# Value products of an attention with mixed heads: three pairs of heads at a time in one PSUM bank, and a third bank for the mixed scores

## The chip, the cores and the metric

One core of a Trainium2 chip runs the whole program. The metric is the device time of one execution in microseconds (us). The engines are named as the profile names them: PE is the matrix engine (PEld its weight loads), DVE the vector engine, ACT the scalar engine, POOL GpSimd, and SP the engine that issues most DMAs. A matmul's result lies in PSUM, which has eight banks; DVE and ACT read it from there.

## The reference, cut to what matters

```python
scores = scale * np.matmul(q, k.transpose(0, 1, 3, 2))     # 2 batches, 12 heads, 448 x 448, depth 64
scores = np.einsum('bhij,hg->bgij', scores, w_pre)         # heads are mixed before the softmax
attn = np.exp(scores - np.max(scores, axis=-1, keepdims=True))
attn = attn / (np.sum(attn, axis=-1, keepdims=True) + 1e-09)
attn = np.einsum('bhij,hg->bgij', attn, w_post)            # and after it
x = np.matmul(attn, v)                                     # 896 tokens x 768
h = x @ w_in1;  g = h * clip(h + 3, 0, 6) / 6;  y = g @ w_out1
h = y @ w_in2;  g = max(h, 0) + alpha * min(h, 0);  out = g @ w_out2
```

Everything is float32. The two feed-forward layers have 2048 hidden columns.

## The kernel before, in words

The tokens are cut into eight sets of 120, 120, 120 and 88 query rows per batch (`tiles`, numbered 0 to 7). A set is worked off in groups of ten rows times twelve heads, 90 groups in all, and a step `p` of the main loop takes a pair of groups (45 pairs, steps 0 to 44; step 45 finishes the last pair). The order of instructions is the order in which the code is written: every engine works its own list off in order, and nothing is rearranged. A step writes:

- PE, `premix(p)`: four matmuls by `w_pre` into two banks `mx` (line 199), row half `r=0` into the first and `r=1` into the second. DVE takes the negated maximum of each bank (`nm`, line 205), ACT the exponential with its sums (`e`, `sm`, line 214).
- PE, `qk`: in steps up to 35 the scores of one pair of heads of a later set (`sc`, line 174, two banks). ACT copies one bank to `S` and DVE the other (line 555). The scores of a set are read back from `S` by rows through DMAs (`pull`).
- DVE, `norm(p)`: reciprocals (lines 221, 222); then `w_post` is scaled by them (`wr`, line 226), by POOL up to step 36 and by DVE from step 37 on.
- PE, `post(p-1)`: 32 small matmuls with the scaled `w_post` (`pt`, line 238, two banks), which ACT copies to `MT` (line 253).
- PE, `av`: the value products (`av`, line 287), one call for a pair of heads of a finished set: eight matmuls. Three pairs share a bank; behind the third, DVE copies the bank to `xT` (line 296). `av_at` says in which step which pair is written.

In between, `also` places the first conversions of the feed-forward weights, which come as 64-bit integers: `conv_abs` and `conv_low` on ACT at the end of steps 16 and 17 (and 24 and 25, 32 and 33), `conv_shift` and `conv_sign` on DVE at the end of steps 18 and 19 (26 and 27, 34 and 35), `conv_round` on POOL. From step 42 on `in_part` brings the first matmuls of the feed-forward layers (line 452). The value products of set 7 follow behind the loop in two runs of three pairs, with six matmuls of `in_part` ahead of each. Then PE runs feed-forward matmuls to the end.

Of the kernel before, what the change touches and what calls it, by code (L numbers as in the profile page):

```python
# [7 lines left out]
F32 = mybir.dt.float32  # L8
# [17 lines left out]
def spread(items, lo, hi):  # L26

    out = {}
    n = max(1, hi - lo)
    for i, it in enumerate(items):  # L30
        out.setdefault(lo + i * n // len(items), []).append(it)
    return out
# [3 lines left out]
def kernel(  # L36
# [16 lines left out]
    _, D, H, S = k.shape  # L53
# [7 lines left out]
    GP = G * H  # L61
# [6 lines left out]
    tiles = []  # L68
# [12 lines left out]
    NTILE, NG = len(tiles), len(groups)  # L81
# [11 lines left out]
    def pool(stack, name, **kw):  # L93
        return stack.enter_context(tc.tile_pool(name=name, reuse_waits="tile", **kw))
# [9 lines left out]
    psA = pool(p_ps, "psA", bufs=1, space=PSUM)  # L104
    psB = pool(p_sc, "psB", bufs=2, space=PSUM, side="right")

    with tc.manual_schedule():
# [21 lines left out]
        def upper(n):  # L129
            return max(n - (Q - Z), 36)  # L130
# [32 lines left out]
        def qk(ti, j, tag="sc"):  # L163
            n = tiles[ti]["n"]
            if j == 0:
                S_t[ti] = s_pool[(NTILE - 1 - ti) % 3].tile([128, H, S], F32, tag="S", name="S")
            pool_ = psB if tag == "sc" else psA
            ps = [pool_.tile([128, 512], F32, tag=tag, bufs=2, name="sc") for _ in range(2)]
            t = q_st[ti]
            k_ = k_st[tiles[ti]["b"]]  # L170
            for o in range(2):
                b = j * n
                for a, z, r in ((b, b + Q, 0), (b + Q, b + Q + upper(n), Q)):
                    nc.tensor.matmul(  # L174
                        ps[o][r:r + z - a, :S], t[D * o:D * o + D, a:z], k_[D * o:D * o + D, j, :],
                        start=True, stop=True,
                    )
            return [(S_t[ti][:Z + n, 2 * j + o, :], ps[o][:Z + n, :S]) for o in range(2)]
# [12 lines left out]
        def premix(p):  # L191
            d = d_buf[p % len(d_buf)]
            ms = []
            for r in range(2):
                ms.append(psA.tile([128, 512], F32, tag="mx", bufs=2, name="mx"))
            for r in range(2):
                for c in range(2):
                    a, z = Q * r, Q + (groups[2 * p + c][3] - G2) * H if r else Q
                    nc.tensor.matmul(  # L199
                        ms[r][Q * c:Q * c + Q, :S], wpre[a:z], d[a:z, c, :], start=True, stop=True  # L200
                    )
            nms = []
            for m in ms:
                nm = late.tile([128, 1], F32, tag="nm", bufs=4, name="nm")
                nc.vector.tensor_reduce(nm, m[:, :S], axis=AX.X, op=ALU.max, negate=True)  # L205
                nms.append(nm)
            mx_t[p] = ms, nms
# [51 lines left out]
        def by_row(dst, src, n):  # L259
            m = n // G * G  # L260
            d, s = dst[..., :m], src[..., :m]
            if len(dst.shape) == 3:
                yield (d.rearrange("p z (x o) -> p z x o", x=G), s.rearrange("p z (o x) -> p z x o", x=G))
            else:
                yield (d.rearrange("p (x o) -> p x o", x=G), s.rearrange("p (o x) -> p x o", x=G))
            if n > m:
                yield dst[..., m:n], src[..., m:n]

        av_ps, whole = {}, []
# [8 lines left out]
        def av(ti, a):  # L278
            T = tiles[ti]
            n = T["n"]  # L280
            if a % 3 == 0:
                av_ps[0] = psA.tile([128, 3, GP], F32, tag="av", bufs=2, name="av")
            p = av_ps[0]
            for t in range(NJ):
                for o in range(2):
                    h = 2 * a + o
                    nc.tensor.matmul(  # L287
                        p[D * o:D * o + D, a % 3, :n], v_t[T["b"], h // HC][:Q + JH, h % HC, t, :],
                        MT[ti][:Q + JH, t, h, :n], start=(t == 0), stop=(t == NJ - 1),
                        skip_group_check=True,  # L290
                    )
            if a % 3 == 2:
                c0 = T["b"] * S + T["i0"]
                x = xT[:, a - 2:a + 1, c0:c0 + n]
                for d, s0 in by_row(x, p[:, :, :n], n):
                    nc.vector.tensor_copy(d, s0)
                if ti >= NTILE - 2:
                    whole.append((a, T["i0"], n, x))

        qk_at, av_at = {}, {}  # L300
        for i in range((NTILE - 1) * (H // 2)):
            p_ = i // 3 - 2 if i < H // 2 else i - H // 2
            qk_at.setdefault(p_, []).append((1 + i // (H // 2), i % (H // 2)))
        for ti in range(NTILE - 1):
            lo = (tiles[ti]["s"] + tiles[ti]["ng"] - 1) // 2 + 2
            hi = tiles[ti + 2]["s"] // 2 + 1 if ti + 2 < NTILE else lo + 4
            for p_, js in spread(list(range(H // 2)), lo, min(hi, lo + H // 2)).items():
                av_at.setdefault(p_, []).extend((ti, a) for a in js)

        P = {}  # L310
        WC = w_in1.shape[2]
# [220 lines left out]
        for c in range(2):  # L532
            a = GH * c
# [3 lines left out]
        for c in range(2):  # L537
            a = GH * c
# [18 lines left out]
        for j in range(H // 2):  # L557
            s_out(qk(0, j, ("sc", "mx")[j % 2]))
# [7 lines left out]
        for i in range(NC):  # L566
            a = 2 * (14 + 8 * i)
# [33 lines left out]
        for p_ in range(-2, NP + 1):  # L601
# [17 lines left out]
            if 0 <= p_ < NP:  # L619
                premix(p_)  # L620
            two = [lambda ti=ti, j=j: qk(ti, j, "mx" if p_ < 0 and j % 2 else "sc") for ti, j in qk_at.get(p_, [])]
            pend = [f() for f in (two if p_ < 0 else two[:1])]
            if 0 <= p_ < NP:
# [26 lines left out]
            for ti, a in av_at.get(p_, []):  # L650
                av(ti, a)
        for a in range(H // 2):
            if a % 3 == 0:
                in_part(p1, 1, x_t, 0, 2 + 2 * (a // 3), 4 + 2 * (a // 3))
            x1_split()
            av(NTILE - 1, a)
# [148 lines left out]
```

## Time and profile before

| what | value |
|---|---|
| median of 3 runs | 656.22 us (654.49 to 659.57) |
| the profiled execution | 653.05 us, of it a span of 651.3 us on the engines |
| PE busy | 635.8 us (98% of the span) |
| ACT, DVE, POOL busy | 348.0, 408.7, 295.1 us |
| granted clock of PE | 1.000 |

The span runs from the first to the last instruction of the engines. Matmuls are pipelined and their ends are modelled, so the busy share of PE does not say that PE is at its peak; whether a stretch goes at PE's pace is read from the distance between like instructions.

### The profile page before, as it was taken

How to read it: one execution, taken by the hardware profiler on the slowest of the kernel's cores; microseconds unless marked ns; L12 is line 12 of the kernel's file. 1: busy time of each engine (PE TensorE's matmuls, PEld its weight loads, DVE VectorE, ACT ScalarE, POOL GpSimd, SP SyncE). 2: the span in 40 equal slices, each digit the busy share in tenths (PEclk: the TensorE clock that was granted, in tenths of full speed). 3: DMA queues.
4: the chain of work that ended last, by engine and by line, in shares of the span. 5: the costliest groups of instructions: out<-in, count | busy, mean ns of one | idle time of the engine just before them, and what ended most of it. 6: DMA issues, size and time to landing. Idle time of an engine off the chain costs nothing.

```text
span 651.3 us, 16021 instructions
## 1 busy us (share of the span) xinstructions
PE 635.8 (98%) x6696; PEld 549.1 (84%) x6696; DVE 408.7 (63%) x640; ACT 348.0 (53%) x644; POOL 295.1 (45%) x240
## 2 busy tenths in 40 slices
PE   7998999999899999999999999999999999999997
PEld 2576676666689999999999999999999999999997
DVE  3765566666536878788634633589999997444401
ACT  4785868777755666655444534444444443444310
POOL 4121131313535454555776455344455556776430
PEclk9999999999999999999999999999999999999999
DMA  5777654845403222333443332223222224445302
GB/s 161 241 230 201 193 142 157 224 164 146 115 2 95 100 98 98 133 109 99 145 136 113 111 126 97 98 76 119 98 98 97 98 97 146 141 142 191 98 0 86
DMA packets 34917, 81.72 MB, mean 125 GB/s; under 512 B 11420, under 2 KB 24988, under 8 KB 34844
## 3 DMA queue, kind: packets, MB, share of 16 engines
q1 hardware_dynamic: 34268, 80.27, 38.7%
q8 instruction: 53, 0.87, 0.6%
q10 hardware_dynamic: 576, 0.41, 0.3%
q14 instruction: 20, 0.16, 0.1%
HBM read 58.65 MB, written 2.75 MB: 94 GB/s over the span
## 4 chain that ended last, share of the span: by engine, by line
PE 84%; issue 5%; POOL 4%; ACT 3%; DVE 1%; DMA 1%; SPq 0%; POOLq 0%; ACTq 0%; DVEq 0%
PE p L452 63%; PE av L287 6%; PE pt L238 5%; PE sc L174 5%; PE mx L199 5%; POOL wb L374 2%; ACT e L214 2%; POOL wlo L385 2%; DMA qst<-in_q_dram 1%; ACT MT L253 1%; DVE nm L205 1%; ACT S L555 0%; DVE sm L221 0%; SPq L189 0%; POOL wr L226 0%
## 5 line engine op out<-in xcount | busy, mean ns | idle before, releaser
L385 POOL TENSOR_TENSOR wlo<-wb,whi 128x768 fp32r<-128x768 f32 x64 | 127.4, 1991 | 130.1 <-ACT whi L379 130.1
L374 POOL TENSOR_TENSOR wb<-wb,wst 128x768 int32<-128x768 int32 x64 | 125.5, 1962 | 81.0 <-DVE wb L367 64.9
L452 PE MATMUL p<-xh,whi 128*128 128x448 f32 x384 | 140.0, 364 | 0.0
L452 PE MATMUL p<-gl,whi 128*128 128x448 f32 x384 | 139.4, 363 | 0.0
L452 PE MATMUL p<-xl,whi 128*128 128x448 f32 x384 | 139.4, 363 | 0.0
L452 PE MATMUL p<-gh,whi 128*128 128x448 f32 x384 | 139.2, 362 | 0.0
L452 PE MATMUL p<-gh,wlo 128*128 128x448 f32 x384 | 138.4, 360 | 0.1
L452 PE MATMUL p<-xh,wlo 128*128 128x448 f32 x384 | 138.3, 360 | 0.0
L359 DVE TENSOR_SCALAR wb<-wb 128x768 f32<-128x768 f32 x64 | 52.9, 827 | 80.6 <-ACT wb L343 80.6
L343 ACT ACTIVATE wb<-wst 128x768 f32<-128x768 f32 x64 | 58.0, 906 | 69.5 <-DMA wst<-in_w_out_dram 50.7
L379 ACT CAST whi<-wb 128x768 fp32r<-128x768 f32 x64 | 53.3, 832 | 48.8 <-PE p L452 30.6
L452 PEld LDWEIGHTS p<-xh,whi 128*128 128x128 f32 x384 | 72.1, 188 | 6.3 <-issue 0.2
L452 PEld LDWEIGHTS p<-gh,whi 128*128 128x128 f32 x384 | 72.1, 188 | 5.7
L214 ACT ACTIVATE e<-mx,nm 128x448 f32<-128x448 f32 x90 | 56.4, 633 | 38.0 <-DVE nm L205 37.5
L452 PEld LDWEIGHTS p<-gh,wlo 128*128 128x128 f32 x384 | 71.8, 187 | 5.6 <-POOL wlo L385 0.5
L452 PEld LDWEIGHTS p<-xh,wlo 128*128 128x128 f32 x384 | 71.8, 187 | 5.1
L226 POOL TENSOR_SCALAR wr<-wpost,sm 128x60 f32<-128x60 f32 x74 | 25.4, 359 | 110.7 <-DVE sm L222 109.0
L452 PEld LDWEIGHTS p<-gl,whi 128*128 128x128 f32 x384 | 72.1, 188 | 3.6
L452 PEld LDWEIGHTS p<-xl,whi 128*128 128x128 f32 x384 | 72.1, 188 | 3.6
L238 PEld LDWEIGHTS pt<-wr,e 60*64 60x64 f32 (+1 forms) x2880 | 53.2, 133 | 22.8 <-issue 13.8
L205 DVE TENSOR_REDUCE nm<-mx 128x1 f32<-128x448 f32 x90 | 52.1, 619 | 30.3 <-PE mx L199 30.3
L367 DVE SCALAR_TENSOR_TENSOR wb<-wst,wb 128x768 uint32<-128x768 uint32 x64 | 67.5, 1055 | 1.1
(50 smaller groups left out, 761.0 us busy)
## 6 DMA issues: line engine op xcount, KB each, us to landing
wst<-in_w_out_dram SPq DMA_DIRECT2D x32, 768.0 KB
wst<-in_w_in_dram SPq DMA_DIRECT2D x27, 768.0 KB
pull<-S SPq DMA_DIRECT2D x88, 210.0 KB
wst<-in_w_in_dram SPq DMA_DIRECT2D x10, 384.0 KB
v<-in_v_dram SPq DMA_DIRECT2D x16, 168.0 KB
out_dram<-o SPq DMA_DIRECT2D x12, 224.0 KB
qst<-in_q_dram SPq DMA_DIRECT2D x8, 180.0 KB
kst<-in_k_dram SPq DMA_DIRECT2D x4, 336.0 KB
```

Source lines behind the costliest of these rows:

```text
L174: nc.tensor.matmul(ps[o][r:r + z - a, :S], t[D * o:D * o + D, a:z], k_[D * o:D * o + D, j, :], start=True, stop=True,)
L205: nc.vector.tensor_reduce(nm, m[:, :S], axis=AX.X, op=ALU.max, negate=True)
L214: nc.scalar.activation(out=e, in_=ms[o][:, :S], func=ACTF.Exp, bias=nms[o], accum_out=sm[:, o:o + 1])
L238: nc.tensor.matmul(ts[c][Q * z:Q * z + m, u:u + GH], e[a:a + GH, j:j + m], wr[a:a + GH], start=True, stop=True,)
L287: nc.tensor.matmul(p[D * o:D * o + D, a % 3, :n], v_t[T["b"], h // HC][:Q + JH, h % HC, t, :], MT[ti][:Q + JH, t, h, :n], start=(t == 0), ...
L343: nc.scalar.activation(t, s[:, :, 1].bitcast(F32), ACTF.Abs)
L359: nc.vector.tensor_scalar(t, t, W_MAX, W_MIN, ALU.min, ALU.max)
L367: nc.vector.scalar_tensor_tensor(u, st_t[i][:, :, 1], 0xC0000000, u, ALU.bitwise_and, ALU.bitwise_or)
L374: nc.gpsimd.tensor_tensor(n, n, st_t.pop(i)[:, :, 0].bitcast(I32), ALU.add)
L379: nc.scalar.copy(hi, b_t[i])
L385: nc.gpsimd.tensor_tensor(lo, b_t.pop(i), w_t[i][0].bitcast(F32), ALU.subtract)
L452: nc.tensor.matmul(p, wt[a], xt[c], start=(first and z == 0), stop=(last and z == 2))
```

## The change

The three pairs of heads that share a bank are written one right behind the other in one step. The first three pairs of a set come in the step in which the first pair came before, the other three in a step two or three later; steps between have no value products. `av` has one bank in place of two, and `mx` three in place of two, which `qk` uses too in the steps before step 0.

```diff
-            ps = [pool_.tile([128, 512], F32, tag=tag, bufs=2, name="sc") for _ in range(2)]
+            ps = [pool_.tile([128, 512], F32, tag=tag, bufs=3 if tag == "mx" else 2, name="sc") for _ in range(2)]
...
-                ms.append(psA.tile([128, 512], F32, tag="mx", bufs=2, name="mx"))
+                ms.append(psA.tile([128, 512], F32, tag="mx", bufs=3, name="mx"))
...
-                av_ps[0] = psA.tile([128, 3, GP], F32, tag="av", bufs=2, name="av")
+                av_ps[0] = psA.tile([128, 3, GP], F32, tag="av", bufs=1, name="av")
...
-            hi = tiles[ti + 2]["s"] // 2 + 1 if ti + 2 < NTILE else lo + 4
-            for p_, js in spread(list(range(H // 2)), lo, min(hi, lo + H // 2)).items():
-                av_at.setdefault(p_, []).extend((ti, a) for a in js)
+            hi = tiles[ti + 2]["s"] // 2 + 1 if ti + 2 < NTILE else lo + 3
+            for p_, a in ((lo, 0), (min(hi - 1, lo + 3), 3)):
+                av_at.setdefault(p_, []).extend((ti, a + x) for x in range(3))
```

Worked out from `av_at`, the steps with value products and the pairs in each are:

| set (rows) | before: step of the pairs 0 to 5 | after: steps of pairs 0 to 2 and 3 to 5 |
|---|---|---|
| 0 (120) | 7, 8, 9, 10, 11, 12 | 7 and 10 |
| 1 (120) | 13, 14, 15, 16, 17, 18 | 13 and 16 |
| 2 (120) | 19, 19, 20, 21, 21, 22 | 19 and 22 |
| 3 (88) | 24, 24, 25, 26, 27, 28 | 24 and 27 |
| 4 (120) | 30, 30, 31, 32, 33, 34 | 30 and 33 |
| 5 (120) | 36, 36, 37, 38, 39, 40 | 36 and 39 |
| 6 (120) | 42, 42, 43, 44, 44, 45 | 42 and 44 |

PE's list around step 13, before: the last product of set 0, step 13, and its one pair of set 1 (v_132 to v_138 are the four buffers of the values).

```order
L287 MATMUL av<-MT,v_138 64x120 x8
L199 MATMUL mx<-pull,wpre 64x448 x4
L174 MATMUL sc<-kst,qst 64x448
L174 MATMUL sc<-kst,qst 60x448
L174 MATMUL sc<-kst,qst 64x448
L174 MATMUL sc<-kst,qst 60x448
L238 MATMUL pt<-wr,e 64x60 x14
L238 MATMUL pt<-wr,e 56x60 x2
L238 MATMUL pt<-wr,e 64x60 x14
L238 MATMUL pt<-wr,e 56x60 x2
L287 MATMUL av<-MT,v_132 64x120 x8
```

PE's list now, from the last nine products of step 13's burst through step 14 to the start of step 15.

```order
L287 MATMUL av<-MT,v_134 64x120 x9
L199 MATMUL mx<-pull,wpre 64x448 x4
L174 MATMUL sc<-kst,qst 64x448
L174 MATMUL sc<-kst,qst 60x448
L174 MATMUL sc<-kst,qst 64x448
L174 MATMUL sc<-kst,qst 60x448
L238 MATMUL pt<-wr,e 64x60 x14
L238 MATMUL pt<-wr,e 56x60 x2
L238 MATMUL pt<-wr,e 64x60 x14
L238 MATMUL pt<-wr,e 56x60 x2
L199 MATMUL mx<-pull,wpre 64x448 x4
```

The products between `pt` and the next `mx` have gone from step 14; PE goes from one step straight to the next.

The same list in an early step with the semaphores that each matmul waits for, before (Activation is ACT, DMAHW a DMA):

```order
L199 MATMUL mx<-pull,wpre 64x448 [waits DMAHW3_49,Activation_49]
L199 MATMUL mx<-pull,wpre 64x448 [waits DMAHW4_49]
L199 MATMUL mx<-pull,wpre 64x448 [waits Activation_49]
L199 MATMUL mx<-pull,wpre 64x448
L174 MATMUL sc<-kst,qst 64x448 [waits Activation_49]
L174 MATMUL sc<-kst,qst 60x448
L174 MATMUL sc<-kst,qst 64x448 [waits DVE_49]
L174 MATMUL sc<-kst,qst 60x448
L238 MATMUL pt<-wr,e 64x60 [waits Activation_49,Pool_49]
L238 MATMUL pt<-wr,e 64x60 [waits Activation_49]
```

And now:

```order
L199 MATMUL mx<-pull,wpre 64x448 [waits DMAHW3_49]
L199 MATMUL mx<-pull,wpre 64x448 [waits DMAHW4_49]
L199 MATMUL mx<-pull,wpre 64x448 [waits Activation_49]
L199 MATMUL mx<-pull,wpre 64x448
L174 MATMUL sc<-kst,qst 64x448 [waits Activation_49]
L174 MATMUL sc<-kst,qst 60x448
L174 MATMUL sc<-kst,qst 64x448 [waits DVE_49]
L174 MATMUL sc<-kst,qst 60x448
L238 MATMUL pt<-wr,e 64x60 [waits Activation_49,Pool_49]
L238 MATMUL pt<-wr,e 64x60 [waits Activation_49]
```

The wait of the first `mx` matmul on ACT is gone; the third one's stays, for an exponential one earlier; the waits of `sc` and `pt` on ACT are as they were.

DVE's list from step 37 to 39, before:

```order
L205 TENSOR_REDUCE nm<-mx 128x1 x2
L221 TENSOR_SCALAR sm<-sm 128x2
L222 RECIPROCAL sm<-sm 128x2
L226 TENSOR_SCALAR wr<-wpost,sm 128x60 x2
L296 COPY xT<-av 128x3x120
L205 TENSOR_REDUCE nm<-mx 128x1 x2
L221 TENSOR_SCALAR sm<-sm 128x2
L222 RECIPROCAL sm<-sm 128x2
L226 TENSOR_SCALAR wr<-wpost,sm 128x60 x2
L205 TENSOR_REDUCE nm<-mx 128x1 x2
```

And now, from the copy at the end of step 36's burst:

```order
L296 COPY xT<-av 128x3x120
L205 TENSOR_REDUCE nm<-mx 128x1 x2
L221 TENSOR_SCALAR sm<-sm 128x2
L222 RECIPROCAL sm<-sm 128x2
L226 TENSOR_SCALAR wr<-wpost,sm 128x60 x2
L205 TENSOR_REDUCE nm<-mx 128x1 x2
L221 TENSOR_SCALAR sm<-sm 128x2
L222 RECIPROCAL sm<-sm 128x2
L226 TENSOR_SCALAR wr<-wpost,sm 128x60 x2
L205 TENSOR_REDUCE nm<-mx 128x1 x2
```

The copy of `xT` has moved from behind step 37 to behind step 36; in both lists a step's maxima stand behind the scaled `w_post` of the step before. The lists of POOL and SP are unchanged, and so is ACT's up to step 42.

## Rows read from the trace of the kernel before

**Rows 1.** Busy time by stretch: steps 7 to 35, steps 36 to 41, feed-forward layers.

```profile
37.40:147.00 109.60, 105.60 (x2802) 73.61 (x2797) 68.14 (x165) 82.09 (x210) 23.80 (x65) 1.00 0.63 185
147.00:168.50 21.50, 19.12 (x531) 13.16 (x535) 13.10 (x38) 17.03 (x44) 9.87 (x10) 1.00 0.58 162
...
193.50:651.30 457.80, 454.16 (x2271) 425.00 (x2268) 294.95 (x362) 209.10 (x296) 240.81 (x122) 1.00 0.32 108
```

**Rows 2.** The chain of waits, step 17 (start us, us, what).

```profile
76.30 0.91 PE mx L199 x8
77.21 0.75 PE sc L174 x8
77.97 0.92 PE pt L238 x60
78.89 0.97 PE av L287 x16
```

**Rows 3.** The chain, value products of two pairs, one pair and three pairs (sets 2, 3, 7).

```profile
95.39 1.79 PE av L287 x32
...
110.42 0.76 PE av L287 x16
...
191.61 1.97 PE av L287 x48
```

**Rows 4.** The chain around step 23, which has no value products.

```profile
102.41 0.92 PE pt L238 x60
103.33 1.09 PE mx L199 x6
104.42 0.84 PE sc L174 x7
105.27 1.21 PE pt L238 x60
106.47 1.36 PE av L287 x32
```

**Rows 5.** The timeline there: start us, us, instruction [idle before <- who ended it].

```profile
102.43 0.63 ACT L214 ACTIVATE e<-mx,nm 128x448 f32<-128x448 f32 x1 [0.86 <-DVE nm L205]
...
103.83 0.20 PEld L199 LDWEIGHTS mx<-pull,wpre 60*64 60x64 f32 x4 [0.42 <-ACT e L214]
...
104.25 0.52 PEld L174 LDWEIGHTS sc<-kst,qst 64*64 64x64 f32 x8 [0.23 <-ACT S L555]
...
104.53 0.61 ACT L253 COPY MT<-pt 120x480 f32<-120x480 f32 x1
...
104.78 1.55 PEld L238 LDWEIGHTS pt<-wr,e 60*64 60x64 f32 x64
...
104.98 0.69 ACT L214 ACTIVATE e<-mx,nm 128x448 f32<-128x448 f32 x1
```

**Rows 6.** ACT's timeline, first exponentials of two steps before step 7.

```profile
27.91 0.64 ACT L214 ACTIVATE e<-mx,nm 128x448 f32<-128x448 f32 x1
...
30.62 0.63 ACT L214 ACTIVATE e<-mx,nm 128x448 f32<-128x448 f32 x1
```

**Rows 7.** The timeline: ACT's conversion at the end of step 17; PE in step 36.

```profile
80.55 0.93 ACT L349 ACTIVATE wst<-wst 128x768 int32<-128x768 uint32 x1
...
149.15 1.15 PE L238 MATMUL pt<-wr,e 60*64 60x60 f32 x64 [0.56 <-POOL wr L226]
```

**Rows 8.** DVE's timeline, the maxima of steps 37 to 40.

```profile
153.06 1.15 DVE L205 TENSOR_REDUCE nm<-mx 128x1 f32<-128x448 f32 x2 [1.70 <-PE mx L199]
...
156.39 1.15 DVE L205 TENSOR_REDUCE nm<-mx 128x1 f32<-128x448 f32 x2
...
159.28 1.15 DVE L205 TENSOR_REDUCE nm<-mx 128x1 f32<-128x448 f32 x2
...
162.59 0.62 DVE L205 TENSOR_REDUCE nm<-mx 128x1 f32<-128x448 f32 x1
```

**Rows 9.** DVE's timeline behind the loop: the copies behind set 7's first three pairs.

```profile
190.25 0.50 DVE L296 COPY xT<-av 128x240 f32<-128x240 f32 x2 [0.71 <-PE av L287]
```

## The prediction

> **What bounds the kernel now.** I first read the busy time by stretch [rows 1]. From 193.50 us on PE is busy for 454.16 of 457.80 us and nothing here touches that part; it moves as a block with the end of the attention. In steps 7 to 35 PE is busy 105.60 of 109.60 us, ACT 82.09; in steps 36 to 41 PE only 19.12 of 21.50, ACT 17.03. The granted clock is 1.00 throughout, so there is no clock to win. Busy shares say little of PE, so the chain of waits comes next. In step 17 it lies on PE alone: mx 0.91, sc 0.75, pt 0.92 and one pair of products 0.97, 3.56 us in all (0.01 is lost in rounding) [rows 2]. Without the products a step is 2.58 us of PE work. Around step 23, which has none, the chain runs from 102.41 to 106.47: 4.06 us for pt, mx, sc, pt, which unstalled are 0.92 + 0.91 + 0.75 + 0.92 = 3.50 [rows 4]. So **a step without products (I call it quiet) costs a stall of 0.56 us**, paid in the step behind it.
>
> The timeline shows why [rows 5]. From one first exponential to the next, 102.43 to 104.98, ACT needs 2.55 us for its own list (two exponentials, a copy of S, the copies to MT), as long as PE needs for a quiet step. Three waits on ACT stand in a row on PE: 0.42 us at 103.83 for an exponential (the mx bank), then sc until the S copy is done (the load at 104.25), then pt, whose 64 loads are stretched to 1.55 us because its second bank is free only when the copy of MT ends at 104.53 + 0.61 = 105.14. With products in the step, PE comes 0.97 us later and meets none of them. Before, steps 7 to 35 have three quiet steps (23, 29, 35).
>
> **The change part by part.** The sum is made against the profiled execution, 653.05 us (span 651.3 and 1.75 around it). That is 3.2 us under the median of 656.22, near the edge of the runs; I add the sum to the median.
>
> *Products in bursts.* Set by set from the table of the change, for sets 0 to 4. A single pair of 120 rows takes 0.97 us [rows 2], two together 1.79 [rows 3], so a pair added to a burst costs 0.82 and three take 1.79 + 0.82 = 2.61 (estimate). Before: 18 singles and 3 doubles, 17.46 + 5.37 = 22.83 us; after: 8 bursts, 20.88; saved 1.95. For 88 rows a burst of three is in the trace, 1.97, a single 0.76 [rows 3], a double 1.36 [rows 4]: set 3 goes from 4 x 0.76 + 1.36 = 4.40 to 3.94, saved 0.46. Together **-2.41**, all of it on PE, which sets the pace there.
>
> *Quiet steps in 7 to 35.* They go from 3 to 19, nearly all in twos: 8 and 9, 11 and 12, and so on, with 23 single. I leave out 34 and 35 (below): nine runs. The third mx bank removes the first of the three waits, since premix then needs the exponential before the last, done 0.6 us earlier. The other two stay: sc would begin at 103.33 + 0.91 = 104.24 and is held until 104.25 anyway; pt would begin at 104.99, and its second matmul is held until 105.14. In the second step of a run ACT's list of 2.55 is no longer than PE's 2.58, so it adds no new backlog, and the burst behind the run lets ACT catch up. Bounds for a run: below, the steady pace of the steps before step 7, which have no products either, 30.62 - 27.91 = 2.71 per step [rows 6], 0.13 over 2.58, so 0.26 for two; above, 0.56 for each, 1.12. I take 0.5, one isolated stall with the little that the third bank takes off. Nine runs are +4.5, less 2 x 0.56 for the old steps 23 and 29: **+3.4** (1.2 to 8.4, the upper end for 17 quiet steps).
>
> *Conversions whose cover goes.* conv_low takes 0.93 us of ACT at the end of step 17 [rows 7], and again in 25. A step with one pair left ACT 3.56 - 2.55 = 1.01 us, which hid it. Both steps are now the first of a quiet run; exponentials, S and MT of the next step come 0.93 later, some of which PE has already lost to the stall of the run. I take 0.6 each, **+1.2** (0 to 1.9). Those of steps 16, 24 and 33 fall into bursts, and that of 32 has a burst behind it: nothing. At 34 and 35 DVE's conversions already delay things: pt of step 36 waits 0.56 us for wr [rows 7]. Step 34 loses its pair of 0.97 us; I take **+0.35** for both steps (0 to 0.97), their quiet run counted in it.
>
> *Steps 36 to 41.* There is no sc here, and the pace is a ring through DVE and ACT: maxima, exponentials, reciprocals, scaled w_post, next maxima. From maxima to maxima it takes 3.33, 2.89 and 3.31 us [rows 8]; the first has the copy of xT in it, the second none, so a quiet turn is 2.89 or so. A single pair hid inside such a turn. A burst doesn't: premix of the next step is queued behind it on PE, DVE's maxima wait for premix, and ACT for those. In step 39 pt (1.15, [rows 7]) + 2.61 + premix (0.91, [rows 2]) and some 0.1 to hand over to DVE (estimate) are 4.8 to 4.9 where 3.31 stood: +1.55. In step 36 the burst replaces a double: +0.82. Two quiet turns lose the copy, 2 x 0.44 = -0.88. Together **+1.5** (0.5 to 2.4).
>
> *Steps 42 to 45.* The six matmuls of in_part keep PE the pace. Two doubles become bursts, +1.64, two singles go, -1.94: **-0.3**.
>
> *One bank for the products.* Bursts of the loop lie two or three steps apart and the copy to xT follows at once. The two bursts behind the loop are the close ones: the copies end at 190.25 + 0.50 = 190.75 [rows 9], the next burst starts at 191.61 [rows 3], covered by 0.86 us of in_part: nothing. If that cover were gone it would be 0.6. The Trainium skill (Perfetto Trace Analysis, Matmuls) says that independent groups of matmuls should rotate through several banks so that evacuation overlaps the next group. By that rule alone giving up the second bank would cost the 0.6 at the end, and the sum would be 4.3; the rows show the evacuation done in time, and I keep 0.
>
> *Third mx bank elsewhere.* Before step 7 it also removes waits of PE, but the pace of 2.71 there goes through ACT and the MT banks: 0 (-0.5 to 0). PE's other idle time in 7 to 35 is part of the 4.0 us of [rows 1] and is left as it is.
>
> Sum: -2.41 + 3.4 + 1.2 + 0.35 + 1.5 - 0.3 = **+3.7 us**: 656.8 on the profiled execution, **659.9** on the median, 0.6% slower.
>
> **The rivals.** *The third bank makes quiet steps free.* For it: the first wait that PE meets at 103.83 is the one for the mx bank, and all that follows could be its echo. Against it: sc and pt wait for ACT's copies by themselves. Then there is no stall in any run and none for the conversions: -2.41 - 1.12 + 1.5 - 0.3 = -2.3, 653.9 us.
>
> *ACT's backlog carries over.* Quiet steps pay 0.56 each because the second of a run meets the MT copy as late as the first: 17 x 0.56 - 1.12 = 8.4, with both conversions in full 1.9. Sum -2.41 + 8.4 + 1.9 + 0.35 + 1.5 - 0.3 = +9.4, 665.6 us, slower than before by over 1%. It decides where ACT's list in a second quiet step is longer than PE's 2.58. Against it: 2.55 at 104.98, and only 0.13 per step in the steady stretch. For it: in that stretch the list was 2.71.
>
> *The ring of steps 36 to 41 has slack that I don't see* and takes the bursts at no cost, the rest as forecast: 3.7 - 1.5 = +2.2, 658.4 us.
>
> **How the numbers follow.** The forecast has a chance of 0.50, the free quiet steps 0.20, the backlog 0.18, the slack in the ring 0.12. The predicted time is the forecast's, 659.9 us. The range reaches from the free quiet steps, 653.9, with the upper part of that case kept, to just short of the backlog: 654.5 to 664.5; what it leaves out is the lower half of the one case and most of the other. A change of 1% (6.6 us) is about what a measurement of this kernel can tell from no change. Faster by that would take the best end of every term, 0.03. Slower by that (above 662.8) is the backlog and a little of the forecast's upper end, 0.20. Within 1%: 0.77.
>
> **What would show it.** Right, if in the profile after the chain around a quiet run stays on PE with pt stretched to 1.1 to 1.3 us in the second step, loads of mx no longer wait for exponentials there while sc and pt wait for S and MT, a burst of 120 rows takes 2.6, and maxima 39 to 40 lie 4.8 apart. From the first maxima of step 7 to the end of step 35 some 2.5 us more should pass, and 1.2 more from 36 to 45. Wrong, if quiet steps are 2.58 apart throughout (then the first rival), if two in a row are 3.1 each (then the second), or if PE's gaps that no wait explains change by several us, since I have left those alone.

## The result, and the profile after

The changed kernel took 660.32 us (median of 16 runs, 652.80 to 663.09), the kernel before beside it 655.28 us. The ratio is **1.0069, with an interval of 1.0041 to 1.0097**: about 4.5 us slower, a change within 1%. The forecast was +3.7 us, 659.9 us, added up on the 656.22 us that were known of the kernel before.

The profiled execution of the changed kernel is the slowest of its 16 (663.09 us, granted clock 0.994), so patterns are read from it and sizes from the experiments as well.

The busy time by stretch, which answers to [rows 1] (steps 7 to 35, steps 36 to 41, feed-forward layers; the columns are us, busy us of PE, PEld, DVE, ACT and POOL with their instructions, granted clock, DMA share and GB/s):

```profile
39.30:155.90 116.60, 108.66 (x2816) 74.82 (x2805) 68.66 (x165) 82.08 (x211) 23.84 (x65) 0.99 0.60 175
155.90:178.70 22.80, 20.19 (x534) 13.30 (x532) 12.97 (x37) 17.07 (x45) 9.45 (x10) 1.00 0.53 146
203.40:661.30 457.90, 454.25 (x2274) 425.05 (x2268) 296.63 (x362) 209.11 (x296) 240.33 (x122) 1.00 0.32 108
```

The feed-forward part moved as a block (457.90 us where 457.80 stood). Steps 7 to 35 grew by 7.0 us in this execution, steps 36 to 41 by 1.3. PE is now idle for 7.9 of 116.60 us, where it was idle for 4.0 of 109.60.

The chain of waits from the end of step 16's burst to the start of step 20, which answers to [rows 2]:

```profile
82.97 1.54 PE av L287 x30
84.50 0.99 PE mx L199 x8
85.49 0.62 DVE nm L205
...
86.19 1.34 ACT e L214 x4
87.53 0.42 ACT S L555
87.96 0.63 ACT MT L253 x2
...
88.75 0.39 ACT wst L349
...
89.56 1.37 ACT e L214 x4
90.93 0.43 ACT S L555
...
91.41 0.98 PE sc L174 x8
92.39 1.09 PE pt L238 x62
93.48 2.61 PE av L287 x48
96.09 0.99 PE mx L199 x8
```

In step 17 the chain lay on PE alone. Now it goes through ACT in the quiet steps: exponentials, the copy of S, the copies to MT, with `conv_low` (L349) in the middle of it, and comes back to PE with the last of the quiet steps. The forecast had named a chain that stays on PE around a quiet run as a sign of being right; that sign did not come. The burst of 120 rows takes 2.61 us, as estimated.

The timeline of the quiet steps 14 and 15, which answers to [rows 5]:

```profile
76.07 0.31 PEld L199 LDWEIGHTS mx<-pull,wpre 64*64 64x64 f32 x8
76.12 1.04 PE L199 MATMUL mx<-pull,wpre 64*64 64x448 f32 x8
...
77.06 1.05 ACT L253 COPY MT<-pt 120x480 f32<-120x480 f32 x2
...
77.23 0.30 PEld L174 LDWEIGHTS sc<-kst,qst 64*64 64x64 f32 x8 [0.85 <-ACT S L555]
77.23 1.08 PE L174 MATMUL sc<-kst,qst 64*64 64x448 f32 x8
...
77.39 0.60 POOL L226 TENSOR_SCALAR wr<-wpost,sm 128x60 f32<-128x60 f32 x2 [10.60 <-DVE sm L222]
77.76 1.34 PEld L238 LDWEIGHTS pt<-wr,e 60*64 60x64 f32 x61 [0.23 <-POOL wr L226]
...
78.03 1.21 PE L238 MATMUL pt<-wr,e 60*64 60x60 f32 x61
...
79.82 0.21 PEld L174 LDWEIGHTS sc<-kst,qst 64*64 64x64 f32 x8 [0.54 <-ACT S L555]
...
80.36 1.40 PEld L238 LDWEIGHTS pt<-wr,e 60*64 60x64 f32 x64 [0.32 <-POOL wr L226]
```

And PE in step 17 of the kernel before, with one pair of products:

```profile
76.23 0.98 PE L199 MATMUL mx<-pull,wpre 64*64 64x448 f32 x8
77.03 0.93 PE L174 MATMUL sc<-kst,qst 64*64 64x448 f32 x8
77.78 1.10 PE L238 MATMUL pt<-wr,e 60*64 60x60 f32 x64
```

The load of `mx` waits for nothing any more here. The load of `sc` waits for the copy of S (0.85 us, then 0.54), and the loads of `pt` are stretched (1.34 and 1.40 us; the forecast had 1.1 to 1.3). But a weight load overlaps the matmuls ahead of it, so its idle time is not yet time that PE loses; that is read from the starts of the matmuls. From `mx` to `sc` they lie 1.11 us apart where they lie 0.80 apart before: the copy of S costs PE some 0.31 us. From `sc` to `pt` it is 0.80 where 0.75 stood, so the 0.23 us for which the first load of `pt` waited for POOL's `wr` cost next to nothing. Behind that, the trace has ACT's second copy to MT end the wait of `pt`'s second bank at 78.12 us, and the next matmul of `pt` starts at 78.16.

The idle time of the weight loads between 36 and 160 us (us in total, times, longest) shows where waits stand, not what they cost PE. Before,

```profile
PEld pt L238 <- POOL wr L226: 2.8, 6, 1.3
PEld mx L199 <- ACT e L214: 2.1, 7, 0.4
PEld sc L174 <- ACT S L555: 1.8, 8, 0.2
```

and after:

```profile
PEld sc L174 <- ACT S L555: 12.8, 18, 0.8
PEld pt L238 <- POOL wr L226: 7.8, 17, 2.0
PEld mx L199 <- ACT e L214: 1.3, 4, 0.4
```

DVE's maxima of steps 37 to 40, which answer to [rows 8]:

```profile
162.77 1.16 DVE L205 TENSOR_REDUCE nm<-mx 128x1 f32<-128x448 f32 x2 [0.39 <-PE mx L199]
165.66 1.15 DVE L205 TENSOR_REDUCE nm<-mx 128x1 f32<-128x448 f32 x2
168.55 1.15 DVE L205 TENSOR_REDUCE nm<-mx 128x1 f32<-128x448 f32 x2
...
173.41 1.16 DVE L205 TENSOR_REDUCE nm<-mx 128x1 f32<-128x448 f32 x2 [0.39 <-PE mx L199]
```

Step 39 to step 40 is 4.86 us (forecast 4.8 to 4.9), and a turn without a burst 2.89.

### The profile page after: what moved, and what is told of

It is laid out like the page before. It is cut to its first block, busy times and chain, and to the rows that moved or that the text cites. A ratio compares the mean times of both kernels' runs of the same rounds, so it can differ in the third digit from the quotient of the medians.

```text
span 661.3 us, 15980 instructions
## 1 busy us (share of the span) xinstructions
PE 640.3 (97%) x6696; PEld 550.0 (83%) x6696; DVE 411.4 (62%) x640; ACT 347.5 (53%) x644; POOL 295.1 (45%) x240
## 4 chain that ended last, share of the span: by engine, by line
PE 79%; issue 5%; POOL 5%; ACT 5%; DMA 3%; DVE 2%; SPq 0%; ACTq 0%; POOLq 0%; DVEq 0%
PE p L452 62%; PE av L287 5%; PE pt L238 4%; PE mx L199 4%; PE sc L174 3%; ACT e L214 3%; POOL wb L374 2%; POOL wlo L385 2%; DVE nm L205 2%; DMA kst<-in_k_dram 1%; DMA pull<-S 1%; DMA qst<-in_q_dram 1%; ACT S L555 1%; ACT MT L253 1%; POOL xl L448 0%
## 5 line engine op out<-in xcount | busy, mean ns | idle before, releaser
L238 PEld LDWEIGHTS pt<-wr,e 60*64 60x64 f32 (+1 forms) x2880 | 54.9, 134 | 31.2 <-issue 13.4
L367 DVE SCALAR_TENSOR_TENSOR wb<-wst,wb 128x768 uint32<-128x768 uint32 x64 | 69.1, 1080 | 1.1
L238 PE MATMUL pt<-wr,e 60*64 60x60 f32 (+1 forms) x2880 | 56.2, 220 | 9.7 <-issue 6.1
```

Of the source, the lines that this page charges most:

```text
L238: nc.tensor.matmul(ts[c][Q * z:Q * z + m, u:u + GH], e[a:a + GH, j:j + m], wr[a:a + GH], start=True, stop=True,)
L367: nc.vector.scalar_tensor_tensor(u, st_t[i][:, :, 1], 0xC0000000, u, ALU.bitwise_and, ALU.bitwise_or)
```

## The experiments

How they are read: the time of all, with its interval, and the start of a step, which is the start of its maxima on DVE. From step to step these starts repeat to 0.05 us between executions where no gap falls in, so a difference of 0.3 us shows there that the time of the whole kernel (interval of some 0.3% to each side) can't show. The twelve kernels were run in three groups of four, each beside runs of the kernel before on the same chip; its medians were 654.92 us (the first four), 654.76 (the next four) and 654.88 (the last four). The ratio is not the plain quotient of two medians (e9: 1.0007 as a quotient, 1.0026 as the ratio), so differences of 0.2% are not read from either. The edits are cut to the lines that matter, those of e1 to e3 to the numbers of banks.

**e1, the bursts with the old banks:** the changed kernel with two `mx` banks and two for the products.

```diff
-  mx: bufs=3   av: bufs=1
+  mx: bufs=2   av: bufs=2
```

> Only the schedule of the bursts, with the banks of before (mx two, products two). My theory (ACT's copies to S and MT set what a quiet step costs, the bank of mx does not): the cycle of two quiet steps and a burst of 120 rows stays near 10.8 us, loads of mx wait 0.4 us for exponentials again, and the whole is within 1 us of the changed kernel, 1.005 to 1.009 of the kernel before. If the third mx bank matters, each of ten quiet runs costs 0.4 more: 11.2 us a cycle and 1.012 to 1.014. If the single bank of the products costs anything, this kernel is faster than the changed one by 0.6 us or more, seen as a gap ahead of bursts in the changed kernel.

660.87 us, ratio 1.0094 (1.0060 to 1.0129). A cycle of a burst and two quiet steps takes 10.93 us, where it takes 10.74 to 10.80 with three banks; steps 23 to 25, with one quiet step, take 8.01 where they take 7.56. The waits stand on `mx` now:

```profile
PEld mx L199 <- ACT e L214: 6.7, 17, 0.4
PEld sc L174 <- ACT S L555: 4.1, 18, 0.2
PEld pt L238 <- POOL wr L226: 2.5, 7, 1.3
```

With the third bank the wait moves from `mx` to `sc` and `pt`, and 0.15 to 0.45 us per quiet run is all that it saves; the 11.2 us a cycle that would have made the bank decisive did not come. The ratio lies a little above the theory's 1.009.

**e2, the banks alone:** the schedule of before with three `mx` banks and one for the products.

```diff
-  mx: bufs=2   av: bufs=2
+  mx: bufs=3   av: bufs=1
```

> Only the banks (mx three, products one), with the schedule of before. My theory: the single bank is copied in time and the third mx bank changes little, the three old quiet steps keep 0.4 to 0.5 of their 0.56 us: 0.998 to 1.001. If the wait for the mx bank is what makes a quiet step slow, those steps become free: -1.7 us, 0.997. If the single bank is waited for, the first pair of a set of three stands behind the copy to xT, some 0.5 us for each of 15: 1.010.

654.65 us, ratio 1.0004 (0.9972 to 1.0036). One bank for the products costs nothing that can be measured. But step 7 starts at 40.01 us where it started at 38.26. This comes back in most kernels with three `mx` banks: after, e2, e5, e7 and e8 start it at 40.01 to 41.32 (only e4 at 38.67), those with two (before, e1, e3, e6, e10) at 38.21 to 39.65.

**e3, the third bank to pt:**

```diff
-  mx: bufs=3   pt: bufs=2
+  mx: bufs=2   pt: bufs=3
```

> The bursts with the spare bank given to pt (three) in place of mx (two). My theory: the second matmul of pt then waits for the first copy to MT and not the second, which ends 0.45 us earlier, so a cycle of two quiet steps and a burst of 120 rows falls from 10.8 to 10.4 or 10.5 us, 3 to 4 us over ten runs: 0.999 to 1.002 of the kernel before. If the mx bank decides, the loss of its third bank makes it slower than the changed kernel, 1.010 or more. If DMAs and late instructions decide, it stays at 1.007.

656.94 us, ratio 1.0045 (1.0013 to 1.0077). A cycle takes 10.92 us, as in e1; steps 23 to 25 take 7.70, between the other two. The 10.4 to 10.5 us of the theory did not come. In a cycle a third bank of `pt` is worth nothing beside two of `mx`, since PE then waits at `mx` (6.6 us of idle weight loads in 17 waits, 6.7 in e1). What it would be worth beside three banks of `mx` no run shows. The ratio is below that of e1, but the two intervals overlap.

**e4, the old end:** the products of sets 5 and 6 where they were before.

```diff
+            if ti < 5:
+                for p_, a in ((lo, 0), (min(hi - 1, lo + 3), 3)):
+                    av_at.setdefault(p_, []).extend((ti, a + x) for x in range(3))
+                continue
+            ... (the places of before)
```

> The changed kernel with the old places of the products for sets 5 and 6. My theory: maxima of steps 39 and 40 lie 3.3 us apart again in place of 4.86, sum over steps 36 to 45 -1.2 us against the changed kernel: 1.004 to 1.006 of the kernel before. If that part has slack, nothing changes: 1.007.

659.13 us, ratio 1.0060 (1.0028 to 1.0093). From step 37 to step 40 it takes 9.53 us again, as before, where the other kernels with bursts there take 10.64 (e3 10.49). In time the 0.6 us against the changed kernel are within the interval.

**e5 and e6, without the loads of the second batch's k:** the changed kernel and the kernel before, each with these four loads left out; the scores of the second batch are computed with the first batch's k.

```diff
-            load_at.setdefault(10 + c, []).append(
-                lambda c=c: load_k(1, c % 2, 3 * (c // 2), 3 * (c // 2) + 3)
-            )
```

> The changed kernel without the loads of the second batch's k in steps 10 to 13 (1.3 MB; both batches use the first k, so the scores of the second batch are not the reference's). A rival that I had left aside: PE's instructions and the pulls of the scores come late where DMAs are dense, and the bursts make that worse in steps 11 to 13 (18.1 us where 10.8 is the plan). If so the stretch falls to 11 or 12 us and the whole by 4 to 6 us, to 0.997 to 1.001 of the kernel before. If these gaps have nothing to do with the loads, the stretch stays at 16 to 18 us and the ratio at 1.007.

> The kernel before without the same loads (the scores of the second batch are not the reference's). DMA rival: its gaps of some 3 us in steps 8 to 13 go, 0.995 to 0.998. What the changed kernel without these loads costs beside it is the price of the schedule alone: by my sum +3.7 us, 1.006 between the two. If the loads don't matter, 1.000.

e5: 654.73 us, ratio 1.0004 (0.9981 to 1.0027). e6: 650.03 us, ratio 0.9938 (0.9911 to 0.9965). By the ratios the loads cost the changed kernel 0.65% (4.3 us) and the kernel before 0.62% (4.1 us): about the same. What lies between the two is still 4.7 us. In e5 steps 11 to 13 take 11.63 us where the changed kernel takes 18.09, as the rival had it. The two traces have fewer gaps than the others and give an accounting: from the start of step 7 to the first feed-forward matmuls behind set 7, 154.77 us in e5 and 151.13 in e6, **+3.64 us**, where the forecast had +3.7; and step 7 starts 1.35 us later. Steps 7 to 35 take 2.4 us more and the rest up to step 45 1.2, where the forecast had 2.5 and 1.2.

What the loads do is seen in the changed kernel's chain of waits, step 12 and the burst of step 13:

```profile
53.67 5.86 DMA pull<-S
...
64.19 0.79 PE pt L238 x45
64.98 3.98 issue
68.96 0.49 PE pt L238 x16
69.45 4.27 PE av L287 x48
```

A pull takes 5.86 us to land. Then PE stands for 3.98 us in the middle of `pt` with no wait for any tile. The DMA queues from 66.00 to 66.50 us show a packet of instructions in this gap (packets, MB, share of 16 engines):

```profile
q8 instruction: 1, 0.02, 16.2%
```

It starts between 66.1 and 66.2 us and takes 0.162 x 16 x 0.5 = 1.3 us; the one ahead of it started between 56.1 and 56.2. Before that they came every 4 to 5 us. PE had stopped at 64.98 and goes on 1.5 us behind the packet's end. The same stands in the other traces: of the 17 gaps over 1 us without a wait between 36 and 195 us, in all kernels, 16 end 1.35 to 1.63 us behind the end of such a packet. So these gaps are waits for instructions, as far as traces can show it. When PE goes on, the granted clock falls (0.50 from 70 to 72 us), and the burst takes 4.27 us where 2.61 is its time. The other kernels with bursts and these loads show gaps at the same place (e1 2.92 us, e4 2.41, e7 4.61, e3 1.42 and 1.73); before has one of 1.86 at 52.0. The loads are not all of it. The changed kernel has a gap of 2.09 us at step 31 and before one of 1.60 at step 41, far from them. And at step 13 each kernel with bursts stands for 0.6 us or more even without these loads or with them spread (e5 0.63, e8 0.66, e9 1.87, e12 0.61), where before, e6, e10 and e11 have no such gap.

**e7, conv_low with conv_abs:** the changed kernel with `conv_low` of blocks 0 and 1 in the step of `conv_abs`, which has a burst.

```diff
-                    at(a + 2 * z, lambda f=f, i=i: f(i))
+                    at(a + 2 * (2 if z == 3 and i < 2 else z), lambda f=f, i=i: f(i))
```

> The changed kernel with conv_low of the first two weight blocks written in the step of conv_abs, a burst step, in place of the quiet steps 17 and 25. My theory: the cycles from step 17 to 20 and from 25 to 28 fall from 11.6 and 10.95 us to 10.8 and 10.15, 1.6 us in all: 1.003 to 1.006 of the kernel before. If the copies for the next steps wait for something else, the cycles stay.

660.15 us, ratio 1.0079 (1.0049 to 1.0110). Steps 17 to 20 take 10.79 us where they take 11.59: the 0.80 are back. Steps 25 to 28 show nothing (11.04 and 10.95 us); in this execution PE's weight loads have a gap of 1.08 us there that no wait explains. The theory is shown for step 17 alone. The ratio missed its 1.003 to 1.006: in time the gain is below what can be seen.

**e8, spread loads:** the changed kernel with the second k in twelve loads of 112 KB in steps 2 to 13, in place of four of 336 KB in steps 10 to 13.

```diff
+        for c in range(H):
+            load_at.setdefault(2 + c, []).append(lambda c=c: load_k(1, c % 2, c // 2, c // 2 + 1))
```

> The changed kernel with the same bytes of the second k in twelve loads of 112 KB in steps 2 to 13, in place of four of 336 KB in steps 10 to 13. DMA rival: the stretch of steps 11 to 13 falls from 18 to 11 or 13 us and the whole by 3 to 6 us: 0.998 to 1.003 of the kernel before. If density of loads is not the cause, 1.007.

656.08 us, ratio 1.0022 (1.0002 to 1.0043): some three quarters of what e5 gained, with nothing left out. The longest time that PE stands without a wait between 36 and 170 us is 0.8 us.

**e9, something to do in step 0:** e8 with four more matmuls behind the first premix, into the third `mx` bank. The start of step 7 with three banks had a likely cause in the clock. Busy time and clock from 20 to 28 us, the changed kernel and e9:

```profile
20.00:28.00 8.00, 8.00 (x149) 4.67 (x149) 4.05 (x11) 3.77 (x9) 1.21 (x4) 0.79 0.57 216
```

```profile
20.00:28.00 8.00, 7.93 (x182) 4.03 (x177) 5.46 (x14) 5.67 (x15) 1.77 (x7) 1.00 0.66 250
```

With two banks PE pauses twice, 0.37 us ahead of the first premix and, in the kernel before, 0.55 us behind it for q. With three the first premix starts without a pause, and PE then stands in one piece until q is there; in the changed kernel it begins again with

```profile
19.80 1.50 PE L174 MATMUL sc<-kst,qst 64*64 64x448 f32 x8 [1.27 <-DMA qst<-in_q_dram]
```

and from 22 to 24 us the granted clock is 0.50.

```diff
+            if p == 0:
+                x = psA.tile([128, 512], F32, tag="mx", bufs=3, name="mx")
+                for c in (0, 1, 0, 1):
+                    nc.tensor.matmul(x[Q * c:Q * c + Q, :S], wpre[:Q], d[:Q, c, :], start=True, stop=True)
```

> The changed kernel with the second batch's k in twelve small loads (656.08 us, 1.0022 beside the kernel before), and in step 0 four more matmuls of the kind of premix behind premix, into the third mx bank; their result is read by nobody. In all four kernels with three mx banks that I looked at, PE stands idle from about 18.4 to 19.7 us for the load of q, then the granted clock is 0.50 from 22 to 24 us, and step 7 begins 1.2 us later than with two banks, where the clock stays 1.00. Theory (the third bank's loss at the start is the clock that falls behind this idle time): with the idle time filled the clock stays 1.00 between 20 and 28 us, the maxima of step 7 start 1.2 to 1.9 us earlier than the 41.3 us of the kernel without the filler, and the time falls by as much, to about 654.6 us, ratio 1.000, although PE has more to do. Rival (the waits of sc and of pt behind three banks cost this time by themselves): the maxima of step 7 start at 41.3 us or up to 0.9 us later, ratio 1.002 to 1.004.

655.35 us, ratio 1.0026 (1.0008 to 1.0045). The trace went by the theory: clock 1.00, and step 3 starts at 27.53 us, 1.25 earlier than in e8 and no later than in the kernels with bursts and two banks (e1 27.92, e3 28.12); step 7 starts at 39.03, 2.3 earlier, the rest of it mostly gaps that e8 has there. The ratio is that of the rival and of e8, so the gain in the trace is not shown in time; the medians, 0.7 us apart, leave room for a part of it. In this execution PE met a gap of 1.87 us between steps 11 and 14 again, for all the spread loads. Nor does the pause alone decide: in e7 it is longer,

```profile
19.99 1.28 PE L174 MATMUL sc<-kst,qst 64*64 64x448 f32 x8 [1.49 <-DMA qst<-in_q_dram]
```

and the clock stays at 1.00, as in e4. So four of six profiled executions with three banks and no filler lost the clock there, none of three with the filler, none of five with two banks. Where it falls, step 3 starts at 28.8 to 29.3 us (e8, e2, e5, the changed kernel), where it doesn't, at 27.9 and 28.4 (e4, e7): 0.4 to 1.4 us later. How often it falls, and with that what it costs on the median, stays open.

**e10, the kernel before with spread loads** (the edit of e8):

> The kernel before with nothing changed but the loads of the second batch's k: twelve of 112 KB in steps 2 to 13 in place of four of 336 KB in steps 10 to 13. Without these loads the kernel before ran in 650.03 us (0.9938). Theory (what costs time in steps 8 to 14 is that the four loads crowd out PE's instructions and the pulls, in both kernels): spread, they cost a quarter of it, as in the changed kernel, about 651.3 us, ratio 0.995. Rival (it is the bytes that cost, whenever they come): ratio 1.000, the gaps of about 3 us in all come in steps 2 to 13 instead.

652.18 us, ratio **0.9965 (0.9942 to 0.9988)**. Faster than both kernels, by 2.7 us against before; the theory had 3.6, and the gain lies between the two expectations, nearer to the theory. It is also the partner of e8: with spread loads the change costs 3.9 us.

**e11, before with the new banks, spread loads and the filler:**

> The kernel before with three mx banks and one for the products (alone 654.65 us, 1.0004), the spread loads, and the four filling matmuls of step 0. Theory by the prediction (a third mx bank takes waits off PE at three quiet steps only and is worth nothing elsewhere): the same time as the kernel before with spread loads, within 0.5 us, ratio 0.994 to 0.996. Rival (the third bank is worth something from step 7 on, and only the fall of the clock at the start hid it when the banks were changed alone): 1.2 to 1.9 us better than with spread loads alone, ratio 0.992.

651.75 us, ratio 0.9974 (0.9948 to 0.9999). The same as e10 within the intervals, and the rival's 0.992 lies outside: with single products the third bank is worth nothing that can be measured from step 7 on either, as the prediction had it.

**e12, the bursts with everything mended:** e9 with `conv_low` of block 0 in the step of `conv_abs`.

```diff
-                    at(a + 2 * z, lambda f=f, i=i: f(i))
+                    at(a + 2 * (2 if z == 3 and i < 1 else z), lambda f=f, i=i: f(i))
```

> The changed kernel with the spread loads, the filling matmuls of step 0, and the first block's conv_low in the step of conv_abs. Theory (what then stays between it and its counterpart with single products is the sum of the prediction from step 7 on, +3.7 us, less 0.8 for conv_low): 2 to 3.5 us slower than the kernel before with the same banks, loads and filler, ratio about 0.998. Rival (bursts cost nothing by themselves, and the start and the loads were all that made the change slower): equal to that kernel within 1 us, ratio 0.994.

656.33 us, ratio 1.0038 (1.0013 to 1.0063). Steps 17 to 20 take 10.78 us, the gain of e7. The time is 4.6 us over e11, more than the 2 to 3.5 of the theory (the two intervals, some 1.6 us to each side, leave room for its upper end), and far from the rival's equality: the bursts cost by themselves.

## Why the prediction was right, and where it was off

The forecast's chain holds: PE saves some work in bursts and loses more in the quiet steps between them, where ACT's list sets the pace. Taking the change apart shows which half costs: the bursts with the old banks 1.0094 (e1), the banks alone 1.0004 (e2). And every like-for-like pair of schedules shows it: e5 against e6 4.7 us, e8 against e10 3.9, e9 against e11 3.6, e12 against e11 4.6, the changed kernel against before 4.5 by the ratio. Term by term, from the starts of the steps (the sum is over steps 7 to 45):

| step of the prediction | forecast | measured |
|---|---|---|
| bursts | -2.41 | burst of 120 rows 2.61, of 88 rows 1.97: -2.41 |
| nine quiet runs, less two old | +3.4 | cycle 10.74 to 10.80 against 3 x 2.58 + 2.61 = 10.35, some 0.42 a run: 9 x 0.42 - 1.12 = +2.7 |
| conv_low in 17 and 25 | +1.2 | steps 17 to 20 11.59 - 10.74 = 0.85; steps 25 to 28 10.95 - (3 x 2.58 + 1.97 + 0.42) = 0.82: +1.7 |
| step 20 | not foreseen | steps 20 to 23 11.08 in e7 against 10.74: +0.3 |
| steps 34, 35 | +0.35 | 7.26 became 6.81, with 0.97 of work gone: +0.5 |
| steps 36 to 41 | +1.5 | the five turns from 36 to 41, 17.22 became 18.51: +1.3 |
| steps 42 to 45 | -0.3 | 42 to 44, 9.85 became 9.56: -0.3 |
| sum | +3.7 | +3.8, and +3.64 directly (e5 against e6) |

**How near the sums lie is partly luck.** The terms miss by -0.7 (quiet runs), +0.5 (conversions), +0.3 (step 20), +0.15 (steps 34 and 35) and -0.2 (steps 36 to 41), and cancel. The 3.64 holds things that no term names: in e5 the gaps of 0.63 us in step 13 and 0.30 in step 22, and a step 41 of 3.50 us where e6 takes 3.06; in e6 a stretch of steps 31 to 33 that takes 12.26 us where its other cycles take 10.68. And 659.9 is near 660.32 because 656.22, the median of three runs, was 0.9 us above the 655.28 of all 16; on that base the forecast is 659.0. What the runs show well is the sign, a price of some 3.6 to 4.7 us, and the terms for the bursts, the conversions and the ring.

**The quiet step.** The mechanism is the one named: ACT's copies hold PE where no products cover them, 0.42 us a run where 0.5 stood. The first quiet step of a run takes 2.45 us, the second 2.93 (steps 14 and 15), so neither 2.58 throughout nor 3.1 each. Within it one size was wrong. The prediction let `sc` wait next to nothing once the `mx` bank is free (104.24 against 104.25); it loses the 0.31 us that stand above, since the wait that the third bank took off `mx` came back at `sc`. `pt` waits for the second copy to MT as the prediction read it, but that costs less: from `pt` to the next `mx` it is 1.01 us (78.03 to 79.04) where it is 0.92 in the quiet step ahead of it, which meets no wait (75.20 to 76.12). No run makes ACT's list shorter in every quiet step; e7 does it in one, by `conv_low`, and PE gets the time back there.

**Step 20.** ACT's first exponential starts 1.00 us behind the start of the maxima of step 20 in every kernel but those with spread loads, which have 0.72 and a step of 2.45 us where the changed kernel takes 2.73. Before has the 1.00 too, where the products cover it. What ACT waits for is open.

**conv_low.** Mis-sized: 0.85 in place of 0.6 in step 17, nearly the whole 0.93, and e7 gave 0.80 of it back. It lies on the chain, since no burst is left in those steps to cover it. Steps 25 to 28 lose the same 0.82, but no run takes `conv_low` cleanly out of them.

**The ring.** The turns came as forecast: step 36 4.23 to 5.05 (+0.82), 37 3.33 to 2.89 (-0.44), 39 3.31 to 4.86 (+1.55); only 40 gained a little more (3.46 to 2.82). The rival with slack there falls.

**One bank for the products.** Nothing, as forecast. At the end the copies are done in time: the burst follows the six matmuls at once,

```profile
200.19 1.41 PE p L452 x6
201.59 1.97 PE av L287 x48
```

and the copies that answer to [rows 9] begin at 200.24 and end at 200.74, 0.85 us ahead of it. The Trainium skill (Perfetto Trace Analysis, Matmuls) says that independent groups of matmuls should rotate through different banks, so that evacuation overlaps the next group; the +0.6 that the prediction worked out for that rule did not come, since here other matmuls cover the copy.

**The rivals.** Free quiet steps: no, a stall is left in every run. The backlog: no, a cycle's stall is 0.42, not twice 0.56.

**What failed** is "third mx bank elsewhere: 0 (-0.5 to 0)". Step 7 starts 1.35 us later in e5 than in e6 and 1.75 later in e2 than in before, and ahead of step 7 these kernels differ in the banks alone. In the traces it goes with the pause for q and, in four of six, with the clock behind it; in the time of e2 (1.0004) it does not show. And the gaps that no wait explains, named as what could make the prediction wrong, did change: at step 13 every kernel with bursts has one, as shown above. But the loads of the second k, which make that gap long in the profile, cost both kernels the same in time (4.3 and 4.1 us by the ratios), so they are not what separates the two. That such gaps can all but cover a change of 1% is why single profiles of these kernels don't show the difference at its size. How the 4.5 us divide between the forecast's terms, the start and the gaps is argued from single traces, not shown by a time.

## What to carry to other kernels

Work that PE does between two waits is cover for the other engines: gathering it into bursts saves its own overhead once and pays for the cover wherever it is taken away, so count the waits of the steps that become empty, and everything (conversions too) that hid in them. A further buffer is worth little where the engine that frees it is itself the pace: here the wait turned up at the next tile. Read what a wait costs from the distance between the matmuls, not from the idle time of their weight loads. And look at when loads are issued, not only whether they are hidden: spreading four loads over twelve steps was worth more here (0.9965) than any change of the schedule that was tried.

## What the runs showed of the hardware

**PE can run out of instructions.** In the changed kernel's profile 52 packets of instructions, 0.85 MB / 52 = 16 KB each, stand among the DMA transfers. With the four loads beside the pulls, one came 10 us behind the last and PE stood for 3.98 us; it went on 1.5 us behind the packet's end, as in 16 of 17 such gaps (1.35 to 1.63). The Trainium skill (Runtime: NRT & Kernel Launch, Instruction fetch mechanics) says that blocks of 16 KiB are fetched ahead and that the cost of crossing from one to the next is mostly hidden. The size agrees; the cost was all but hidden in e8 (no gap over 0.8 us), and not in the changed kernel, e1, e4 and e7 (2.4 to 4.6 us), nor in e9, e10 and e11 with spread loads (up to 1.9, 2.9 and 2.3).

**DVE and POOL are slower beside each other.** In e5, POOL's two `wr` of step 26 take 1.06 us where they take 0.60, beside a conversion of DVE, and DVE's 128 x 2 elements 0.42 where they take 0.17, until POOL's conversion ends at 95.82:

```profile
112.36 0.60 POOL L226 TENSOR_SCALAR wr<-wpost,sm 128x60 f32<-128x60 f32 x2 [4.36 <-DVE sm L222]
...
115.55 0.54 DVE L359 TENSOR_SCALAR wb<-wb 128x768 f32<-128x768 f32 x1
115.80 1.06 POOL L226 TENSOR_SCALAR wr<-wpost,sm 128x60 f32<-128x60 f32 x2 [2.84 <-DVE sm L222]
```

```profile
93.97 1.85 POOL L374 TENSOR_TENSOR wb<-wb,wst 128x768 int32<-128x768 int32 x1
...
95.47 0.42 DVE L221 TENSOR_SCALAR sm<-sm 128x2 f32<-128x2 f32 x1 [0.51 <-ACT e L214]
```

The Trainium skill (SBUF — State Buffer, Who interferes with whom) says that DVE, in some of its modes, and GpSimd contend for a pair of ports which the first to issue holds for its whole instruction. That fits both rows; no run here takes the two apart. Neither delay shows in PE's time: from `sc` to `pt` it is 0.80 and 0.81 us behind them, as in other quiet steps.

**The clock falls behind a pause of PE in some executions and not in others.** Behind a pause of 1.27 us in the changed kernel the granted clock is 0.50, its level of 1.2 GHz, from 22 to 24 us; behind one of 1.49 us in e7, whose instructions are the same up to there, it stays at 1.00. Step 3 starts 0.4 to 1.4 us later where it fell. One execution of each kernel was profiled, so what decides it is open.
